# One core, clustered attention and two MLP stages: products of p and v in runs of four units instead of two

## The chip, the cores and the metric

The kernel runs on one core of one Trainium2 chip. The metric is the device time of one execution in microseconds (us). Three executions of the kernel before took 770.06, 773.00 and 773.85 us, a median of 773.0 us. The profile is of one more execution, which took 773.44 us.

## The reference

Attention over 2 batches of 8 heads, 768 queries and keys of width 64, masked by clusters; then a stage of four matrix products, then a stage of two with a leaky activation. Cut to what matters:

```python
scores = q @ k.T / 8                      # per batch and head, 768 x 768
scores = where(q_cluster == k_cluster, scores, -1e9)
p = exp(scores - max(scores))             # row by row
x = (p / sum(p)) @ v                      # 768 x 64 per head
x = x, heads side by side                 # 1536 x 512
h = ((x @ w1) * (x @ w2)) @ w3 @ w_out
g = h @ w_in;  g = max(g, 0) + alpha * min(g, 0)
out = g @ w_out2
```

The inputs are fp32. Products that must keep fp32 precision are done as three fp32r products of high and low halves (`mm3`), or as fp32 matmuls.

## The kernel before, in words

Attention is cut into 96 **units** (`NU`): unit i is 128 queries of one head against all 768 keys, six units to a head, so two heads' outputs share one tile of x. Two units with the same head in sequence make a **pair** g = i // 2. One loop (L762) over i from 0 to 103 writes the order of work of all engines by hand, as a software pipeline. Each engine runs its own instructions in the order in which the loop emits them. In iteration i:

- TensorE: `emit_T(i-4)`, six 128x128 transposes of p through PSUM tiles `t` (two tiles of three transposes, L551); `emit_S(i+1)`, four matmuls of the scores (L511, L512) into one of two `s` tiles; in some iterations a step of filling work (below); and at the end of each even iteration from 6 on `emit_PV(g)` with g = (i-6)/2: 12 products, 24 matmul instructions in the trace (L568). These have 64-column weights, and the two units of the pair sit in the two column halves of the array (`tile_position`). They accumulate in the one tile `o`, which has a PSUM bank of its own.
- ScalarE (ACT): in odd iterations from 7 on first `emit_x((i-7)//2)`, a copy of the pair's first 64 partitions of `o` into x (L580); then `emit_evac(i-4)`, the copy of the first `t` tile (L558); then `emit_exp(i)`, exp with its row sums (L526).
- VectorE (DVE): the other half of `emit_x` (L581), in even iterations `emit_r` (L533, L534: reciprocals of the row sums of a pair), the copy of the second `t` tile (L559), and `emit_max(i+1)` (L519).
- GpSimd (POOL): `emit_norm(i-2)` (L537), which scales p by the reciprocals; at the first unit of each head also the split of the next head's q and k (`h_split`, L470 to L475).
- SyncE (SP) issues the DMAs, in order: the pieces of `h_split` (L481 to L490), `v_load` (L456) behind the last pair of every second head, the weights (L142, L153), and the raw data of the mask jobs (`j_load`, L314).

A **step of filling work** is one step of `fill_steps` (L699). Up to iteration 55 these steps are the cluster mask jobs (`job`, L316): squares on ACT (L327), products (L337, L346), a sqrt (L374), transposes (L365, L381, L406), a maximum and compares on DVE (L390, L396). They come in every iteration up to 23, in odd ones up to 39, in every one from 41 to 55. From iteration 57 on, in odd iterations, they are steps of the first product with w1 and w2 for the first batch (`l1`): twelve matmuls, with a copy on ACT (L627) behind steps of w1 and a product on DVE (L631) behind steps of w2. In even iterations `w_goal` may add one step of the conversion of a weight: ACT (L185, L196, L280), DVE (L198), POOL (L281).

What limits the run-ahead: `t` has two tiles and both are used in each iteration, so `emit_T(i-3)` needs the copies of `emit_evac(i-4)`; `s` has two tiles, so `emit_S(i+2)` needs `emit_exp(i)`. The transposed p (`pth`) has three buffers of a pair each. `v` has two.

After the loop come the rest of the first product for the first batch, that of the second batch, and the later stages, which the change does not touch.

Of the kernel before, what the change touches and what calls it, by code (L numbers as in the profile page):

```python
# [8 lines left out]
F32 = mybir.dt.float32  # L9
# [7 lines left out]
B, H, S, D, NCL = 2, 8, 768, 64, 16  # L17
P = 128
# [10 lines left out]
def kernel(  # L29
# [14 lines left out]
    nc = tc.nc  # L44

    cp = ctx.enter_context(tc.tile_pool(name="cp", bufs=1))
# [258 lines left out]
    def pst(tag, shape, name, bufs=1):  # L305
        return ps.tile(shape, F32, tag=tag, name=name, bufs=bufs)
# [146 lines left out]
    def v_load(p):  # L453
        if p < B * 4:
            VS[p] = ap.tile([P, 2, NT, D], F32, tag="vs", bufs=2, name=f"vs{p}")
            nc.sync.dma_start(out=VS[p], in_=vv[p // 4, p % 4])  # L456
# [39 lines left out]
    NU = B * H * NT  # L496
    scp, pt, sums, pth, ob, XR = {}, {}, {}, {}, {}, {}

    def unit(i):
        return i // NT, i % NT  # L500
# [21 lines left out]
    def emit_exp(i):  # L522
        if i % 2 == 0:
            sums[i // 2] = ap.tile([P, 2], F32, tag="sums", bufs=3, name=f"su{i}")
        p = ap.tile([P, S], F32, tag="p", bufs=6, name=f"p{i}")
        nc.scalar.activation(  # L526
            out=p.rearrange("p (a k) -> p a k", a=2), in_=scp.pop(i)[:, :, 0:HS], func=AF.Exp,
            bias=nmax.pop(i), scale=1.0, accum_out=sums[i // 2][:, i % 2 : i % 2 + 1],
        )
        pt[i] = p  # L530
# [30 lines left out]
    def emit_PV(g):  # L561

        u, qt = unit(2 * g)
        ob[g] = pst("o", [P, P], f"o{g}")
        v = VS[u // 2]
        for kt in range(NT):
            for j in range(2):
                nc.tensor.matmul(  # L568
                    ob[g][64 * j : 64 * j + 64], lhsT=v[:, u % 2, kt], rhs=pth[g][:, kt, j * P : j * P + P],
                    start=(kt == 0), stop=(kt == NT - 1), tile_position=(0, 64 * j),  # L570
                )

    def emit_x(g):
        u, qt = unit(2 * g)
        o = ob.pop(g)
        p = u // 2
        if u % 2 == 0 and qt == 0:
            XR[p] = cp.tile([P, S], F32, tag=f"xr{p % 4}", name=f"xr{p}")
        mine = slice(0, 64) if u % 2 == 0 else slice(64, 128)
        nc.scalar.copy(out=XR[p][mine, qt * P : qt * P + P], in_=o[0:64])  # L580
        nc.vector.tensor_copy(XR[p][mine, qt * P + P : qt * P + 256], o[64:128])  # L581
        pth.pop(g)


    def lc(f, alloc, between):
# [49 lines left out]
    with tc.manual_schedule():  # L635
# [22 lines left out]
        for j in range(2):  # L658
            nc.vector.tensor_scalar(
                out=cpd[:, j], in0=ct, scalar1=cn2, scalar2=evod[:, j : j + 1], op0=ALU.mult, op1=ALU.mult  # L660
            )
        t = pst("s", [P, 2, 512], "cnt", bufs=2)[:, 0]
# [99 lines left out]
        for i in range(NU + 8):  # L762
            if 0 <= i - LT < NU:
                emit_T(i - LT)
            if i + 1 < NU:
                emit_S(i + 1)

            if i >= 7 and i % 2 == 1 and (i - 7) // 2 < NU // 2:
                emit_x((i - 7) // 2)
            if i >= 2 and i % 2 == 0 and i // 2 - 1 < NU // 2:  # L770
                emit_r(i // 2 - 1)
            if 0 <= i - 2 < NU:
                emit_norm(i - 2)
            if 0 <= i - LT < NU:
                emit_evac(i - LT)
            if i + 1 < NU:
                emit_max(i + 1)
            if i < NU:
                emit_exp(i)
                u, j = unit(i)  # L780
                for k in ((0,), (1, 2), (3, 4), (), (5,), ())[j]:
                    h_split(u + 1, k)
            if i >= NU or i % 2 == 1 or i < 24 or 40 < i < 56:
                if fill_at[0] < (L1_B if i < NU else L1_D):
                    if next(fill) is not None:
                        fill_at[0] += 1
            fine[0] = i < NU - 1
            if 10 <= i < 54 and i % 2 == 0:
                w_goal(at["l1", 0, 2, 0])
            if NUH + 8 <= i < NU - 1 and i % 2 == 0:  # L790
                w_goal(at["l1", 0, fill_at[0] // 4, 0] + 3)
            if NUH + 4 <= i < NUH + 8:
                x_split(0, i - NUH - 4, 0)
                x_split(0, i - NUH - 4, 1)
                xdone.append(i)
            if i == NU - 1:
                late.append(i)
                for k in range(2):
                    w = st_tile(f"wo{k}").rearrange("p a n -> p (a n)").rearrange("p (g t n) -> p g t n", g=3, t=2)
                    for g in range(3):  # L800
                        WO[3 * k + g] = w[:, g, 0], w[:, g, 1]
            if i >= NU - 1:
                w_goal(at["wo", 0, 3, 0])

            k = i - 6
            if k >= 0 and k % 2 == 0 and k // 2 < NU // 2:
                emit_PV(k // 2)
                if k % 12 == 10:
                    v_load(k // 12 + 2)
        pscope.close()  # L810


# [59 lines left out]
        for b, a in ((0, 0), (0, 1), (1, 0), (1, 1)):  # L872
            s = slice(a * HS, a * HS + HS)
            for e in range(4):
                t = alloc_c(f"l2_{b}{e}{a}")
# [323 lines left out]
```

## Time and profile before

| | |
|---|---|
| median of three executions | 773.0 us (770.06 to 773.85) |
| the profiled execution | 773.44 us |
| its span, first to last instruction | 771.6 us |
| TensorE (PE) busy | 746.4 us, 97% |
| its weight loads (PEld) busy | 675.7 us, 88% |
| VectorE busy | 464.6 us, 60% |
| ScalarE busy | 458.0 us, 59% |
| GpSimd busy | 270.1 us, 35% |
| share of the chain that ended last on PE | 86% |
| granted TensorE clock, mean | 0.99 |

The profiled execution is 0.44 us over the median. Between its span and its time lie 1.8 us. A row of the timeline gives the start in us from the first instruction, the length in us, engine, line, operation, output and inputs, shapes and how many instructions were merged; in brackets stands how long the engine was idle before it, and what ended that. Matmuls overlap: the distance from one start to the next is what one costs, not its length.

### The profile page before, as it was taken

How to read it: one execution, taken by the hardware profiler on the slowest of the kernel's cores; microseconds unless marked ns; L12 is line 12 of the kernel's file. 1: busy time of each engine (PE TensorE's matmuls, PEld its weight loads, DVE VectorE, ACT ScalarE, POOL GpSimd, SP SyncE). 2: the span in 40 equal slices, each digit the busy share in tenths (PEclk: the TensorE clock that was granted, in tenths of full speed). 3: DMA queues.
4: the chain of work that ended last, by engine and by line, in shares of the span. 5: the costliest groups of instructions: out<-in, count | busy, mean ns of one | idle time of the engine just before them, and what ended most of it. 6: DMA issues, size and time to landing. Idle time of an engine off the chain costs nothing.

```text
span 771.6 us, 13292 instructions
## 1 busy us (share of the span) xinstructions
PE 746.4 (97%) x5025; PEld 675.7 (88%) x5025; DVE 464.6 (60%) x807; ACT 458.0 (59%) x946; POOL 270.1 (35%) x244
## 2 busy tenths in 40 slices
PE   5899999989999999999999999999999999999998
PEld 2787788879999989999999999999989998989886
DVE  3776798995666674357233446525645547776764
ACT  5687887675556675467344657647565544555443
POOL 0366576684555643243222432312211111221110
PEclk9799999999999999999999999999999999999999
DMA  7657466253534635756444497756655226433402
GB/s 251 193 177 224 108 173 166 67 123 79 150 110 135 186 119 168 236 217 223 160 164 164 161 316 251 282 181 231 206 201 164 110 110 232 177 114 135 163 0 82
DMA packets 39440, 129.41 MB, mean 168 GB/s; under 512 B 5232, under 2 KB 5360, under 8 KB 39376
## 3 DMA queue, kind: packets, MB, share of 16 engines
q1 hardware_dynamic: 39376, 128.56, 51.5%
q8 instruction: 40, 0.66, 0.3%
q14 instruction: 24, 0.20, 0.1%
HBM read 86.17 MB, written 28.31 MB: 148 GB/s over the span
## 4 chain that ended last, share of the span: by engine, by line
PE 86%; DMA 5%; DVE 3%; POOL 2%; ACT 2%; issue 1%; SPq 1%; POOLq 0%; ACTq 0%; DVEq 0%
PE o L568 6%; PE t L551 6%; PE l L298 6%; PE l L299 6%; PE acc L300 6%; PE acc L299 6%; PE l L300 6%; PE acc L298 6%; PE s L511 3%; PE s L512 3%; PE l1a L299 3%; PE l1b L298 3%; PE l1a L298 3%; PE l1a L300 3%; PE l1b L300 3%; PE l1b L299 3%
## 5 line engine op out<-in xcount | busy, mean ns | idle before, releaser
L281 POOL TENSOR_TENSOR wh<-wt,wh 128x512 fp32r<-128x512 f32 x57 | 74.2, 1301 | 169.7 <-ACT wh L280 165.0
L537 POOL TENSOR_SCALAR p<-p,su 128x768 f32<-128x768 f32 x96 | 88.4, 929 | 91.8 <-DVE su L534 42.4
L198 DVE SCALAR_TENSOR_TENSOR wt<-wu,wt 128x512 uint32<-128x512 uint32 x72 | 72.9, 1013 | 40.9 <-ACT wt L196 40.7
L519 DVE TENSOR_REDUCE nm<-s 128x1 f32<-128x768 f32 x96 | 91.5, 953 | 8.6 <-PE s L512 3.1
L526 ACT ACTIVATE p<-s,nm 128x768 f32<-128x768 f32 x96 | 87.1, 907 | 6.8 <-DVE nm L519 5.4
L551 PE MATMUL t<-cst,p 128*128 128x128 f32 x576 | 84.1, 281 | 3.6 <-DVE pt L559 1.6
L551 PEld LDWEIGHTS t<-cst,p 128*128 128x128 f32 x576 | 65.9, 143 | 15.8 <-issue 7.9
L511 PE MATMUL s<-st 128*128 128x384 f32 x192 | 74.9, 390 | 2.0 <-ACT p L526 1.5
L568 PE MATMUL o<-pt,vs 128*64 128x128 f32 x1152 | 73.5, 277 | 0.0
L568 PEld LDWEIGHTS o<-pt,vs 128*64 128x64 f32 x1152 | 61.9, 137 | 12.3 <-issue 12.1
L512 PE MATMUL s<-st 80*128 80x384 f32 x192 | 66.7, 347 | 0.2 <-DMA st<-mk 0.2
L558 ACT COPY pt<-t 128x384 f32<-128x384 f32 x96 | 45.9, 478 | 30.4 <-PE t L551 29.4
L559 DVE COPY pt<-t 128x384 f32<-128x384 f32 x96 | 52.8, 550 | 16.1 <-PE t L551 15.1
L244 POOL TENSOR_TENSOR sp<-sx,sp 128x512 fp32r<-128x512 f32 x16 | 22.4, 1420 | 107.9 <-ACT sp L241 107.5
L968 DVE SCALAR_TENSOR_TENSOR gr<-gr,alp 128x384 f32<-128x384 f32 x32 | 20.9, 652 | 49.1 <-ACT gr L967 49.1
L196 ACT ACTIVATE wt<-wr 128x512 uint32<-128x512 uint32 x72 | 48.3, 671 | 0.0
L185 ACT ACTIVATE wu<-wr 128x512 f32<-128x512 f32 x72 | 47.9, 666 | 0.0
L298 PE MATMUL l1a<-xs,wh 128*128 128x384 f32 x128 | 43.3, 338 | 1.3 <-DVE pr L631 0.7
L280 ACT CAST wh<-wt 128x512 fp32r<-128x512 f32 x57 | 35.4, 621 | 13.1 <-DVE wt L198 7.1
L298 PE MATMUL l1b<-xs,wh 128*128 128x384 f32 x128 | 43.1, 337 | 0.0
L299 PE MATMUL l1a<-xs,wh 128*128 128x384 f32 x128 | 43.0, 336 | 0.1
L631 DVE TENSOR_TENSOR pr<-l1b,asb 128x384 f32<-128x384 f32 x32 | 17.8, 555 | 42.1 <-PE l1b L300 24.3
(244 smaller groups left out, 1984.9 us busy)
## 6 DMA issues: line engine op xcount, KB each, us to landing
wr<-in_w_dram SPq DMA_DIRECT2D x48, 512.0 KB, 5.3
kept<-wh SPq DMA_DIRECT2D x41, 512.0 KB, 5.8
wh<-kept SPq DMA_DIRECT2D x39, 512.0 KB, 4.0
wr<-in_w3t_dram SPq DMA_DIRECT2D x16, 512.0 KB, 4.1
ywc<-kept SPq DMA_DIRECT2D x15, 512.0 KB, 3.5
jm<-in_qka_dram SPq DMA_DIRECT2D x12, 512.0 KB, 5.6
hr<-in_qkh_dram SPq DMA_DIRECT2D x16, 384.0 KB, 3.6
st<-st SPq DMA_DIRECT2D x16, 384.0 KB, 3.7
```

Of the source, the lines that this page charges most:

```text
L198: nc.vector.scalar_tensor_tensor(out=t, in0=u, scalar=3, in1=t, op0=ALU.logical_shift_left, op1=ALU.bitwise_or)
L281: nc.gpsimd.tensor_tensor(out=lo, in0=tts.pop(n), in1=f32(hi), op=ALU.subtract)
L298: nc.tensor.matmul(o, lhsT=whi, rhs=xhi, start=first, stop=False)
L299: nc.tensor.matmul(o, lhsT=whi, rhs=xlo, start=False, stop=False)
L300: nc.tensor.matmul(o, lhsT=wlo, rhs=xhi, start=False, stop=last)
L511: nc.tensor.matmul(t[:, a, 0:HS], lhsT=s[:, 0, q], rhs=s[:, 1, ks], start=True, stop=False)
L512: nc.tensor.matmul(t[:, a, 0:HS], lhsT=s[0:80, 2, q], rhs=s[0:80, 3, ks], start=False, stop=True)
L519: nc.vector.tensor_reduce(out=m, in_=scp[i][:, :, 0:HS], op=ALU.max, axis=AX.XY, negate=True)
L526: nc.scalar.activation(out=p.rearrange("p (a k) -> p a k", a=2), in_=scp.pop(i)[:, :, 0:HS], func=AF.Exp, bias=nmax.pop(i), scale=1.0, acc ...
L537: nc.gpsimd.tensor_scalar(out=pt[i], in0=pt[i], scalar1=sums[i // 2][:, i % 2 : i % 2 + 1], scalar2=1.0, op0=ALU.mult, op1=ALU.mult)
L551: nc.tensor.transpose(t[:, k], pt[i][:, kt * P : kt * P + P], ident)
L568: nc.tensor.matmul(ob[g][64 * j : 64 * j + 64], lhsT=v[:, u % 2, kt], rhs=pth[g][:, kt, j * P : j * P + P], start=(kt == 0), stop=(kt == N ...
```

## The change

`emit_PV` of two pairs, that is of four units, comes at the end of every fourth iteration (8, 12, ... 100) in place of one pair at the end of every second. Both pairs write halves of one `o` tile. `emit_x` is called once per run, in the iteration after it, and copies both pairs with one instruction per engine where they are of one head (16 of the 24 runs) and with two where they are of two (8 runs). In that iteration `emit_exp(i)` is emitted ahead of `emit_x` and `emit_evac`. `v_load` stays in the same iterations.

```diff
     def emit_PV(g):
 
         u, qt = unit(2 * g)
-        ob[g] = pst("o", [P, P], f"o{g}")
+        if g % 2 == 0:
+            ob[g // 2] = pst("o", [P, 2, P], f"o{g}")
         v = VS[u // 2]
         for kt in range(NT):
             for j in range(2):
                 nc.tensor.matmul(
-                    ob[g][64 * j : 64 * j + 64], lhsT=v[:, u % 2, kt], rhs=pth[g][:, kt, j * P : j * P + P],
+                    ob[g // 2][64 * j : 64 * j + 64, g % 2], lhsT=v[:, u % 2, kt], rhs=pth[g][:, kt, j * P : j * P + P],
                     start=(kt == 0), stop=(kt == NT - 1), tile_position=(0, 64 * j),
                 )
 
-    def emit_x(g):
-        u, qt = unit(2 * g)
-        o = ob.pop(g)
-        p = u // 2
-        if u % 2 == 0 and qt == 0:
-            XR[p] = cp.tile([P, S], F32, tag=f"xr{p % 4}", name=f"xr{p}")
-        mine = slice(0, 64) if u % 2 == 0 else slice(64, 128)
-        nc.scalar.copy(out=XR[p][mine, qt * P : qt * P + P], in_=o[0:64])
-        nc.vector.tensor_copy(XR[p][mine, qt * P + P : qt * P + 256], o[64:128])
-        pth.pop(g)
+    def emit_x(n):
+        o = ob.pop(n)
+        parts = []
+        for k in range(2):
+            u, qt = unit(4 * n + 2 * k)
+            p = u // 2
+            if u % 2 == 0 and qt == 0:
+                XR[p] = cp.tile([P, S], F32, tag=f"xr{p % 4}", name=f"xr{p}")
+            x = XR[p][0:64] if u % 2 == 0 else XR[p][64:128]
+            parts.append((u, x.rearrange("p (t q) -> p t q", q=P), qt, k))
+            pth.pop(2 * n + k)
+        if parts[0][0] == parts[1][0]:
+            (_, x, qt, _) = parts[0]
+            parts = [(x[:, qt : qt + 4].rearrange("p (k j) q -> p k j q", j=2), slice(0, 2))]
+        else:
+            parts = [(x[:, qt : qt + 2].rearrange("p (k j) q -> p k j q", j=2), slice(k, k + 1)) for _, x, qt, k in parts]
+        for x, k in parts:
+            nc.scalar.copy(out=x[:, :, 0], in_=o[0:64, k])
+        for x, k in parts:
+            nc.vector.tensor_copy(x[:, :, 1], o[64:128, k])
...
-            if i >= 7 and i % 2 == 1 and (i - 7) // 2 < NU // 2:
-                emit_x((i - 7) // 2)
+            if i % 4 == 1:
+                if i < NU:
+                    emit_exp(i)
+                if i >= 9:
+                    emit_x((i - 9) // 4)
...
             if i < NU:
-                emit_exp(i)
+                if i % 4 != 1:
+                    emit_exp(i)
...
-            k = i - 6
-            if k >= 0 and k % 2 == 0 and k // 2 < NU // 2:
-                emit_PV(k // 2)
-                if k % 12 == 10:
-                    v_load(k // 12 + 2)
+            if i % 4 == 0 and 8 <= i < NU + 8:
+                for g in (i // 2 - 4, i // 2 - 3):
+                    emit_PV(g)
+                    if g % 6 == 5:
+                        v_load(g // 6 + 2)
```

## Rows read from the trace of the kernel before

**Rows 1.** Windows of the attention loop: us, busy us (instructions) by engine, clock, DMA

```profile
39.00:172.00 133.00, 124.98 (x1268) 106.44 (x1267) 110.14 (x208) 103.77 (x227) 89.10 (x86) 1.00 0.55 150
172.00:275.00 103.00, 103.00 (x898) 95.68 (x897) 66.05 (x126) 60.00 (x136) 55.79 (x55) 1.00 0.50 135
```

**Rows 2.** Timeline of PE, 273.7 to 280 us, iterations 89 to 91

```profile
273.75 0.93 PE L568 MATMUL o<-pt,vs 128*64 128x128 f32 x14
...
275.86 0.34 PE L512 MATMUL s<-st 80*128 80x384 f32 x1
276.05 0.82 PE L551 MATMUL t<-cst,p 128*128 128x128 f32 x6
276.63 0.44 PE L511 MATMUL s<-st 128*128 128x384 f32 x1
...
277.26 0.34 PE L512 MATMUL s<-st 80*128 80x384 f32 x1
277.52 1.53 PE L568 MATMUL o<-pt,vs 128*64 128x128 f32 x24
278.99 0.88 PE L551 MATMUL t<-cst,p 128*128 128x128 f32 x6
279.62 0.42 PE L511 MATMUL s<-st 128*128 128x384 f32 x1
```

**Rows 3.** Line 568, then line 551's first idle entry: durations, idle us and times

```profile
L568 PE MATMUL o<-pt,vs x1152: 272/273/324, 39.4 to 306.9; 128*64 128x128 f32 x192
...
  issue: 12.1, 47
...
  issue: 7.9, 40
```

**Rows 4.** Lines 580 and 581, the copies of x: min/median/max ns

```profile
L580 ACT COPY xr<-o x48: 238/258/261, 41.0 to 307.4; 64x128 f32<-64x128 f32 x48
...
L581 DVE COPY xr<-o x48: 292/294/296, 41.3 to 307.7; 64x128 f32<-64x128 f32 x48
```

**Rows 5.** Timeline of PE: five waits, in iterations 12, 19, 24, 32 and 44

```profile
53.28 0.64 PE L337 MATMUL ja<-jm,cst 128*32 128x256 f32 x8 [0.46 <-ACT jm L327]
...
75.68 0.64 PE L337 MATMUL ja<-jm,cst 128*32 128x256 f32 x8 [1.46 <-ACT pr L352]
...
90.27 0.44 PE L511 MATMUL s<-st 128*128 128x384 f32 x1 [0.90 <-ACT p L526]
...
109.00 0.55 PE L551 MATMUL t<-cst,p 128*128 128x128 f32 x3 [0.70 <-DVE pt L559]
...
139.73 0.55 PE L406 MATMUL jd<-cst,pr 128*128 128x128 f32 x3 [0.87 <-DVE pr L396]
```

**Rows 6.** Timelines of ACT, SP and DVE: what stands behind these waits

```profile
52.17 1.06 ACT L327 ACTIVATE jm<-jm 128x1024 f32<-128x1024 f32 x1 [0.37 <-DMA jm<-in_qka_dram]
...
67.33 0.33 SPq L456 DMA_DIRECT2D vs<-in_vv_dram  x1
...
74.09 1.06 ACT L327 ACTIVATE jm<-jm 128x1024 f32<-128x1024 f32 x1 [2.71 <-DMA jm<-in_qka_dram]
...
87.93 1.28 ACT L526 ACT_TABLE_LOAD   x1
...
106.74 1.29 DVE L198 SCALAR_TENSOR_TENSOR wt<-wu,wt 128x512 uint32<-128x512 uint32 x1
...
138.32 1.82 DVE L396 TENSOR_TENSOR pr<-pr,mx 128x384 f32<-128x384 f32 x2
```

**Rows 7.** Timelines of PE and ACT, iteration 66, behind a step of w1

```profile
200.87 0.82 PE L551 MATMUL t<-cst,p 128*128 128x128 f32 x6
...
202.02 0.47 ACT L558 COPY pt<-t 128x384 f32<-128x384 f32 x1
202.38 0.91 ACT L526 ACTIVATE p<-s,nm 128x768 f32<-128x768 f32 x1
```

**Rows 8.** Timeline of DVE, iteration 90: the copy of the second `t` tile

```profile
277.40 0.54 DVE L559 COPY pt<-t 128x384 f32<-128x384 f32 x1
```

## The prediction

> **What bounds the kernel now.** I read the windows first, to see how much room each stage has, then the timeline of TensorE, then what ended its waits.
>
> In the loop's first part (39 to 172 us, iterations 6 to 56) TensorE is busy 124.98 of 133 us, with VectorE at 110.14 and ScalarE at 103.77: three engines close together, and 8.0 us in which TensorE waits. In the second part (172 to 275 us, filled up with steps of w1 and w2) it is busy all 103.00 us, and VectorE only 66.05 [rows 1]. TensorE sets the pace; in the first part its partners are just behind. The granted clock is 1.00 in both, its upper level.
>
> The timeline shows what one run of PV costs. S ahead of T starts its last matmul 0.19 us before T (275.86 to 276.05); ahead of PV it is 0.26 (277.26 to 277.52). PV to the next T is 1.47 (277.52 to 278.99). T to S is 0.63 behind PV and 0.58 elsewhere [rows 2]. Inside a run, 14 instructions last 0.93 us and one lasts 0.273, so seven pairs have six distances of 0.11 us, and twelve pairs stream in 1.31 us [rows 2, 3]. A run that stands alone therefore takes 0.07 + 1.47 + 0.05 = 1.59 us for 1.31 us of streaming. The other **0.28 us** is getting into the 64-column arrangement and out again.
>
> The Trainium skill, "TensorEngine Tiling (Array Packing)", section "Key Properties", says that changing the tiling mode (not just the tile) drains the engine. If each change let one matmul run out, that would be 2 x (0.273 - 0.11) = 0.33 us, an estimate by that page's rule, and 24 such changes would be worth 7.9 us. The trace agrees in kind, and gives the smaller number.
>
> **The change part by part.** The profiled execution is the basis, 773.44 us, 0.44 above the median.
>
> *Fewer runs.* 48 runs become 24. 24 x 0.28 = **-6.7 us**, if TensorE is never kept waiting longer. Bounds: nothing, if the pause belongs to the start of each pair's accumulation rather than to the switch (no row shows two pairs in sequence); and 24 x (12.1/47 + 7.9/40) = 24 x 0.455 = -10.9 us, if all of the weight loader's idle time around runs went [rows 3]. I take the first, since it is the distance between starts on the pacing engine.
>
> *The copies of x.* ACT's 48 copies of 0.258 us become 32, DVE's 48 of 0.294 likewise [rows 4]. A copy twice as wide lies between one and two of these. Both engines gain something between 0 and 4.7 us (16 x 0.294) over the loop, off the path except where named below. In the split runs two copies follow each other, which puts the copy of `t` back by under 0.1 us. Taken as nothing.
>
> *exp ahead of x.* In iterations 1, 5, 9, ... exp(i) no longer stands behind the wait for PV and for T; its maximum was emitted an iteration before, so it runs under the double run, which lasts 2.8 us. Without this move x would hold exp up by the second half of the run. On the path I count nothing: what TensorE asks of ACT next is the copy of `t`, which stands behind x as before.
>
> *One bank, buffers, queues.* The next run writes `o` four iterations after x has read it. pth has three buffers; a run frees two, and the next is written two iterations on. Both hidden. v_load follows the same pair as before. What is queued behind it on SP still waits for the end of that run; POOL keeps its order. The last run is in iteration 100 as before, and TensorE has filling work there, so what the loop gains or loses is the kernel's.
>
> *The cover that moves.* This is the price. The loop had T S T S PV; now it has T S T S T S T S and PV twice. Of four iterations, call them A, A+1, A+2, A+3 (A the one after a run), the PV that stood at the end of A+1 is now at the end of A+3. It covered 1.6 us in which ACT and DVE did A+1's work before TensorE asked for it in A+2 and A+3. Wherever TensorE waits in A+2 or A+3 for something on a clock of its own, it now arrives 1.59 us earlier, waits that much longer, and does the PV afterwards.
>
> - *Five such waits stand in the trace*, all in A+2 or A+3, 0.46 to 1.46 us each [rows 5]. The square at 52.17 waits for a DMA. The one at 74.09 waits 2.71 us for a DMA that was queued on SP behind v_load, and v_load, at 67.33, for the end of a run. exp(23) stands behind a table load at 87.93. The copy of `t` that T waits for at 109.00 stands behind a weight conversion of 1.29 us, and L406 behind two compares that took 1.82 [rows 6]. If all wait the full 1.59 longer: +8.0. In the last four a copy of x (0.26 or 0.29) leaves the delaying engine's queue: -1.1. **+6.9 us.** Lower bound nothing, if the delayed work moves ahead with TensorE.
> - *The second part.* Eight groups have a step of w1 in A. In A+1 ACT then first does that step's copy, and in five of the eight a weight conversion, so that the copy of `t` starts 1.15 us after T (200.87 to 202.02) and ends at 202.49; exp ends at 203.29 [rows 7]. With no PV there, the next T would start at 200.87 + 0.58 for T + 0.82 for S (276.63 to 277.26 and 0.19) = 202.27 [rows 2]. It waits to some 202.5, and the S behind it, due at 203.1, to some 203.4 for exp. That is +0.6 in each of the five, and I take 0.1 in the other three: **+3.3 us**. Bounds: 0, and 8 x 0.6 = 4.8.
> - *The other eleven groups.* Iteration 90 is the pattern. The reciprocals delay the copy of `t` to 277.40, and it ends at 277.94 [rows 8]. With no PV, T would start at 277.26 + 0.19 = 277.45 and its second half 0.29 later, so it waits 0.2. I add as much for the exponential behind it. Against this, DVE and ACT have 1.3 us more to catch up under the double run, and of the present short waits some go. I take 0.25 per group, **+2.8 us**; bounds 0 and 0.4.
>
> Sum: -6.7 + 6.9 + 3.3 + 2.8 = +6.3; 773.44 + 6.3 = 779.7, against the median 773.0 + 6.3 = 779.3. I say **779.0 us**.
>
> The conversion and the compares on DVE that stand behind two of the waits took 1.29 and 1.82 us [rows 6]; each has two SBUF inputs. The Trainium skill, "GPSIMD Engine Reference", section "1. Specifications", says that GpSimd shares its SBUF interfaces with VectorE and that they contend where a VectorE instruction has two SBUF inputs. By it these stretches hang on what POOL does at the time and would not shrink when TensorE comes sooner; the rows quoted show their lengths, not POOL's part in them.
>
> **The rivals.** What a measurement of this kernel can tell from no change is about 0.5%, 3.9 us.
>
> - *The cover was not needed.* DVE and ACT catch up under the double run, the five waits follow TensorE, and the slack in A+2 and A+3 is over 1.6 us. Then only the first term is left: 773.0 - 6.7 = 766.3 us. For it: in the second part VectorE is busy 64% of the time [rows 1]. Against it: the waits that are there [rows 5] and ACT's lateness behind a step of w1 [rows 7]. It decides the sign from the point where extra waits stay under 6.7 us in all, 0.28 per group. Chance 0.14.
> - *The five waits do not grow*, because what TensorE waits for is itself released by TensorE's earlier instructions, but the other two prices are right: -6.7 + 3.3 + 2.8 = -0.6, 772.4 us. Or they grow by half: 775.8. For it: L396 and the compares depend on transposes of an iteration before. Against it: a DMA, a table load and a conversion do not. Chance 0.30.
> - *The run has no gain to give.* The pause comes with each pair's new accumulation, so a double run costs 3.2 us in place of 2.9. Then the waits alone are left: 773.0 + 13.0 = 786 us. Against it: T starts a new tile after three transposes without a pause in its 0.58 us [rows 2]. Chance 0.04.
>
> **How the numbers follow.** My forecast has 0.52, by itself 776 to 784. Faster by over 0.5% is the first rival, 0.14; within 0.5% the second, 0.30; slower the forecast and the third, 0.56. The range goes from 769.5, which leaves out most of the first rival, to 784.5, which leaves out the third and the upper tail of the forecast.
>
> **What would show it.** Right: runs of 48 matmuls with one pair distance of 0.11 between the two pairs; S to PV still 0.26, PV to T twice 1.31 plus 0.16; L568's idle on issue 23 times, some 6 us; TensorE's waits at L337, L406 and at the T and S of A+2 and A+3 grown by 1 us and more; S of A+2 waiting for exp in five groups of the second part; DVE's wait for ACT's copy of x fewer. Wrong: the second part shorter than before by 2 us or more, or the five waits no longer than they were, or a pause in the middle of a run.

## The result: 1.2% slower, and the profile after

| | before | after |
|---|---|---|
| median | 772.48 us (4 runs) | **781.66 us** (4 runs) |
| lowest, highest | 770.06, 773.85 | 780.62, 782.83 |
| ratio, 95% interval | | **1.0123** [1.0092, 1.0154] |
| span of the profiled execution | 771.6 | 779.3 |
| TensorE busy in it | 746.4 of 771.6 | 744.8 of 779.3 |

The changed kernel is slower by 9.2 us. TensorE's busy time hardly moved, and the span grew: most of the loss is waiting.

The windows of the changed kernel (window, length, then busy time of PE, PEld, DVE, ACT, POOL, granted clock, DMA share, GB/s), beside [rows 1]:

```profile
0.00:39.00 39.00, 25.65 (x197) 16.21 (x197) 22.04 (x48) 25.71 (x49) 11.10 (x17) 1.00 0.71 220
39.00:172.00 133.00, 120.50 (x1196) 102.86 (x1196) 99.96 (x189) 97.56 (x207) 81.49 (x80) 0.99 0.53 145
172.00:275.00 103.00, 101.16 (x882) 94.25 (x883) 66.42 (x122) 59.71 (x133) 58.06 (x57) 1.00 0.49 130
```

In the loop's first part TensorE waits 133.00 - 120.50 = 12.5 us where it waited 8.0. In the second part, where it had waited for nothing, it now waits 1.84 us.

A better ruler than windows is the distance between first transposes (T) of a group, iterations A to A+3, because it doesn't slide when the loop is late. Worked out from the starts of the T rows of both traces, in us:

| groups of iterations | before | after | difference |
|---|---|---|---|
| the five with a wait priced in the prediction: 9-12 | 10.35 | 11.45 | +1.10 |
| 17-20 | 14.34 | 14.73 | +0.40 |
| 21-24 | 11.07 | 13.81 | +2.73 |
| 29-32 | 9.99 | 10.81 | +0.82 |
| 41-44 | 10.53 | 11.85 | +1.31 |
| second part with a step of w1, five of eight (65-68, 73-76, 77-80, 81-84, 85-88) | 12.88 each | 13.17 to 13.28 | +0.29 to +0.40 each |
| the other three (57-60, 61-64, 69-72) | 12.88 each | 12.69 to 12.70 | -0.18 to -0.19 each |
| ten others: 5-8, 13-16, 25-28, 33-36, 37-40, 45-48, 49-52, 53-56, 89-92, 93-96 | | | +0.60, +0.12, +0.53, -0.11, +0.45, +0.10, +0.68, -0.89, +0.87, +0.45 |

From the first T of iteration 9 to that of iteration 97 the loop grew by 9.7 us. The two profiled spans differ by only 7.7, because the changed kernel's loop starts 2.4 us earlier (T of iteration 5 at 33.02, before at 35.46): in the profiled execution of before, TensorE ran part of the first 39 us at a lower clock, 0.82 on average against the 1.00 above:

```profile
0.00:39.00 39.00, 27.35 (x185) 19.37 (x186) 20.39 (x45) 24.11 (x45) 8.72 (x14) 0.82 0.70 220
```

**What the change was made of did happen.** TensorE's timeline in iteration 68 of the changed kernel (start, duration, engine, line, operation, tiles, shape, count):

```profile
212.54 0.34 PE L512 MATMUL s<-st 80*128 80x384 f32 x1
212.80 2.84 PE L569 MATMUL o<-pt,vs 128*64 128x128 f32 x48
215.57 0.88 PE L551 MATMUL t<-cst,p 128*128 128x128 f32 x6
...
  issue: 6.4, 24
```

The last line is from the view of what the weight loader waited for at L569. A run of 48 lasts 2.84 us, against 1.53 for one of 24: the second pair adds 1.31, exactly its streaming time, so there is no pause in the middle. S to the run is 0.26 as before. The weight loader idles 24 times, 6.4 us in all, where it idled 47 times and 12.1 us [rows 3]. So the switches that were to go are gone.

**Where the time went.** TensorE's waits of the changed kernel at the five places of [rows 5], with those just beside them and the run behind one of them (in brackets: us waited, what ended it):

```profile
51.22 0.64 PE L337 MATMUL ja<-jm,cst 128*32 128x256 f32 x8 [0.62 <-ACT jm L327]
74.28 0.64 PE L337 MATMUL ja<-jm,cst 128*32 128x256 f32 x8 [2.23 <-ACT pr L352]
87.65 0.98 PE L551 MATMUL t<-cst,p 128*128 128x128 f32 x6 [1.01 <-ACT pt L558]
89.86 0.44 PE L511 MATMUL s<-st 128*128 128x384 f32 x1 [1.23 <-ACT p L526]
91.04 4.16 PE L569 MATMUL o<-pt,vs 128*64 128x128 f32 x48
108.99 0.55 PE L551 MATMUL t<-cst,p 128*128 128x128 f32 x3 [1.02 <-DVE pt L559]
111.54 0.55 PE L551 MATMUL t<-cst,p 128*128 128x128 f32 x3 [0.62 <-DVE pt L559]
141.40 0.55 PE L551 MATMUL t<-cst,p 128*128 128x128 f32 x3 [0.66 <-ACT pt L558]
143.91 0.55 PE L406 MATMUL jd<-cst,pr 128*128 128x128 f32 x3 [1.26 <-DVE pr L396]
```

L337 waits 0.62 (before 0.46) and 2.23 (1.46), S of iteration 24 waits 1.23 (0.90) with a new wait of 1.01 just ahead of it, T of iteration 32 (at 111.54) waits 0.62, a little less than before (0.70), with a new 1.02 in T of iteration 31 ahead of it (at 108.99), and L406 waits 1.26 (0.87) with a new 0.66 ahead of it. What held them up (ACT, then DVE):

```profile
72.70 1.06 ACT L327 ACTIVATE jm<-jm 128x1024 f32<-128x1024 f32 x1 [2.44 <-DMA jm<-in_qka_dram]
...
87.52 1.28 ACT L526 ACT_TABLE_LOAD   x1
88.82 0.90 ACT L526 ACTIVATE p<-s,nm 128x768 f32<-128x768 f32 x1
...
105.28 0.43 DVE L593 COPY xr<-o 64x256 f32<-64x256 f32 x1 [1.45 <-ACT xr L591]
...
107.19 1.02 DVE L396 TENSOR_TENSOR jm<-jm,mx 128x384 f32<-128x384 f32 x2
...
108.40 0.54 DVE L559 COPY pt<-t 128x384 f32<-128x384 f32 x1
```

Iteration 24 shows the mechanism best. The changed kernel comes to the transposes of L381 at 86.15, where before was there at 87.98, since the run that before had at 85.1 to 86.6 is missing: 1.8 us sooner. The exponential behind its table load starts at 88.82 and lets S go at 89.86, where before's S started at 90.27 [rows 5]: 0.4 us sooner. The other 1.4 us have gone into the waits of 1.01 and 1.23, and the run is still to be done. At 108.99 it is a copy of `t` again, but one an iteration earlier. It stands behind two compares (107.19), which before ran at 104.21, mostly under the run of iteration 30 that is now missing, and these behind a copy of x that waited 1.45 us for ACT's. And in the group 9-12 only 0.16 us are at L337; another 0.54 is a wait of S for the transfer of a mask, which before doesn't have.

In the second part, iteration 66 is the pattern that the prediction drew from [rows 7]. TensorE, then ACT:

```profile
205.88 0.82 PE L551 MATMUL t<-cst,p 128*128 128x128 f32 x6
207.44 0.84 PE L551 MATMUL t<-cst,p 128*128 128x128 f32 x6
208.45 0.44 PE L511 MATMUL s<-st 128*128 128x384 f32 x1 [0.16 <-ACT p L526]
...
206.08 0.48 ACT L638 COPY asb<-l1a 128x384 f32<-128x384 f32 x1 [2.67 <-PE l1a L300]
206.46 0.68 ACT L185 ACTIVATE wu<-wr 128x512 f32<-128x512 f32 x1
207.04 0.47 ACT L558 COPY pt<-t 128x384 f32<-128x384 f32 x1
207.40 0.91 ACT L526 ACTIVATE p<-s,nm 128x768 f32<-128x768 f32 x1
```

The copy of `t` stands behind w1's copy and a conversion and starts 207.04 - 205.88 = 1.16 us after T, as before (1.15). T to the next T is 1.56 here, against 1.40 (0.58 for T and 0.82 for S) where nothing is late, and S waits 0.16 for the exponential.

The other way round it shows at T of iteration 57, which stands behind a run and waits for POOL's normalization (before, then the changed kernel):

```profile
171.58 0.88 PE L551 MATMUL t<-cst,p 128*128 128x128 f32 x6 [1.13 <-POOL p L537]
...
176.97 0.88 PE L551 MATMUL t<-cst,p 128*128 128x128 f32 x6 [0.26 <-POOL p L537]
```

With a second pair in the run ahead of it the wait is 0.87 us shorter; the group 53-56, which ends with it, is the one that got 0.89 shorter.

### The profile page after: what moved, and what is told of

It is laid out like the page before. It is cut to its first block, busy times and chain, and to the rows that moved or that the text cites. A ratio compares the mean times of both kernels' runs of the same rounds, so it can differ in the third digit from the quotient of the medians.

```text
span 779.3 us, 13249 instructions
## 1 busy us (share of the span) xinstructions
PE 744.8 (96%) x5025; PEld 673.9 (86%) x5025; DVE 459.2 (59%) x791; ACT 455.0 (58%) x930; POOL 269.8 (35%) x244
## 4 chain that ended last, share of the span: by engine, by line
PE 83%; DVE 7%; ACT 4%; DMA 3%; issue 1%; POOL 1%; SPq 1%; ACTq 0%; DVEq 0%
PE o L569 7%; PE l L298 6%; PE l L299 6%; PE acc L300 6%; PE acc L299 6%; PE l L300 6%; PE acc L298 6%; PE t L551 5%; PE l1a L299 3%; PE l1b L298 3%; PE l1a L298 3%; PE l1a L300 3%; DVE nm L519 3%; PE l1b L300 3%; PE l1b L299 3%; PE s L511 3%
## 5 line engine op out<-in xcount | busy, mean ns | idle before, releaser
L569 PE MATMUL o<-pt,vs 128*64 128x128 f32 x1152 | 69.5, 278 | 0.0
L569 PEld LDWEIGHTS o<-pt,vs 128*64 128x64 f32 x1152 | 63.7, 139 | 6.4 <-issue 6.4
L559 DVE COPY pt<-t 128x384 f32<-128x384 f32 x96 | 52.6, 548 | 11.1 <-PE t L551 10.1
L638 ACT COPY asb<-l1a 128x384 f32<-128x384 f32 x32 | 15.3, 479 | 51.1 <-PE l1a L300 51.1
```

The lines of the kernel that those rows point to most:

```text
L569: nc.tensor.matmul(ob[g // 2][64 * j : 64 * j + 64, g % 2], lhsT=v[:, u % 2, kt], rhs=pth[g][:, kt, j * P : j * P + P], start=(kt == 0), s ...
```

## The experiments

Theory: the switches are worth some 0.28 us each; the PV of A+1, moved to the end of A+3, was cover for late partners of TensorE, and the waits that it uncovers cost more than the switches give. Rivals: the price lies in the copies of x or in the exponential put ahead of them; or in the five waits alone.

### Two iterations later

```diff
-            pth[g] = ap.tile([P, NT, 256], F32, tag="pth", bufs=3, name=f"pt{g}")
+            pth[g] = ap.tile([P, NT, 256], F32, tag="pth", bufs=4, name=f"pt{g}")
...
-            if i % 4 == 0 and 8 <= i < NU + 8:
-                for g in (i // 2 - 4, i // 2 - 3):
+            if i % 4 == 2 and 10 <= i < NU + 8:
+                for g in (i // 2 - 5, i // 2 - 4):
```

Against the changed kernel; the exponential and the copies of x that went first in 4n+1 go first in 4n+3.

> The changed kernel with its double runs two iterations later: pairs 2n and 2n+1 at the end of iteration 4n+10 in place of 4n+8, x and the early exp in the iteration after; pth gets a fourth buffer, since a pair now stays two iterations longer. Theory (cover): the five fixed waits of iterations 12, 19, 24, 32 and 44 then stand in the first or second iteration behind a double run, which is done ahead of them, so they do not grow; the steps of w1 in iterations 57, 61, ... come two iterations behind a run and their late copy of t is covered by the next one. The 6.7 us of fewer switches stay, less some 2 us of other short waits: 767 to 771 us, second part 2 us shorter than before, no stretch at the half clock. Rival (any double run starves TensorE, since T S four times over is faster than ACT and DVE can follow, wherever it is put): 779 to 783 us, as the changed kernel. Rival (the switch costs nothing on the path): 773 us.

Measured: 778.21 us, 1.006 [1.004, 1.0079] of before. The five groups with the priced waits came to -0.9 us together against before (in the changed kernel +6.4), and seven groups of the second part took 12.65, 0.23 less than before. So far the theory. But the time missed, since other groups of the first part got longer: 25-28 by 1.9, 37-40 by 1.4, 53-56 by 0.9. TensorE's timeline, and the window behind it:

```profile
174.31 0.87 PE L551 MATMUL t<-cst,p 128*128 128x128 f32 x6 [2.08 <-POOL p L537]
...
175.60:179.00 3.40, 3.40 (x12) 3.40 (x11) 1.38 (x4) 0.67 (x2) 2.91 (x4) 0.50 0.62 118
```

T of iteration 57 waits 2.08 us for POOL's normalization: with no run ahead of it the wait that was 1.13 and 0.26 lies bare. The granted clock is then 0.50 for 3.4 us, and the group that starts there is 1.3 longer than before. Moving the runs moves the cover, and what it leaves bare depends on the place: the first part has such steps at both places tried.

### The filling shifted by one

```diff
-            if i >= NU or i % 2 == 1 or i < 24 or 40 < i < 56:
+            if i != 57 and (i >= NU or i % 2 == 1 or i < 24 or 40 < i < 56):
```

Against the changed kernel: the steps of w1 come two iterations later in their groups, with the run's cover behind them.

> The changed kernel with one edit: the step of filling work of iteration 57 is left out there, so every step of w1 and w2 moves two iterations back, and steps of w1 with their copy on ACT fall in iterations 59, 63, ... (third of a group, covered by the double run of the fourth). Theory: the five groups of the second part that became 0.34 us longer become 0.19 shorter like the other three: 5 x 0.53 = 2.7 us less than the changed kernel, about 779 us; iteration 66's copy of t starts 0.6 us behind T. Rival (these groups are longer for DVE's sake, or for three steps without PV as such): as the changed kernel, 781.7.

Measured: 779.93 us, 1.0088 [1.0068, 1.0108]. All seven groups from 61 to 88 take 12.69, where the changed kernel has 13.17 to 13.28 in five of them. The timeline of TensorE and ACT in iteration 70:

```profile
220.27 0.82 PE L551 MATMUL t<-cst,p 128*128 128x128 f32 x6
...
220.85 0.48 ACT L558 COPY pt<-t 128x384 f32<-128x384 f32 x1 [3.05 <-PE t L551]
```

The copy of `t` now starts 0.58 us after T, in place of 1.16. So the excess of the five groups goes with that delay. The conversions move with the steps of w1, so which of the two delays the copy more isn't told apart. The other 0.19 per group below before is what fewer switches give here. Some of the gain is lost again behind it: the group 89-92 is 1.2 us longer than in the changed kernel.

### The exponential back behind the copies of x

```diff
             if i % 4 == 1:
-                if i < NU:
-                    emit_exp(i)
                 if i >= 9:
                     emit_x((i - 9) // 4)
...
             if i < NU:
-                if i % 4 != 1:
-                    emit_exp(i)
+                emit_exp(i)
```

> The changed kernel with exp(i) of iterations 1, 5, 9, ... back behind x and the copy of t, as it was before. Theory: exp would then start about 1.0 us behind T in place of under the double run, its s tile comes free at 1.9 us, and S of the next iteration, due at 2.0 us, waits by 0 to 0.2 us: 0 to +4 us on the changed kernel, 782 to 786 us. Rival (the move itself is what costs, since x and the copy of t wait behind exp): 2 us or more faster than the changed kernel, under 780.

Measured: 781.95 us, 1.0121 [1.0098, 1.0145]: the changed kernel again. With double runs the order of exp and x is worth nothing that can be told, either way.

### The copies and the exponential without the double runs

```diff
-            if i % 4 == 0 and 8 <= i < NU + 8:
-                for g in (i // 2 - 4, i // 2 - 3):
-                    emit_PV(g)
-                    if g % 6 == 5:
-                        v_load(g // 6 + 2)
+            if i % 2 == 0 and 6 <= i < NU + 6:
+                g = i // 2 - 3
+                emit_PV(g)
+                if g % 6 == 5:
+                    v_load(g // 6 + 2)
```

Against the changed kernel: single runs where before had them, shared tile of `o`, x copied every fourth iteration, early exponential.

> The change without its merged runs: one pair per run at the end of every second iteration as before, but both pairs in one o tile, x copied once per two runs and exp(i) ahead of it in every fourth iteration. Theory (the run's place is all): as before, 770 to 774 us, faster by at most 1 us for 16 copies less on each engine; the five waits as long as before. Rival (the wide copy, the shared tile or the early exp costs): 775 us or more.

Measured: 780.25 us, 1.0094 [1.0076, 1.0113], a miss of 6 us. The timeline of ACT, DVE and TensorE in iteration 9:

```profile
44.81 0.90 ACT L526 ACTIVATE p<-s,nm 128x768 f32<-128x768 f32 x1 [1.39 <-DVE nm L519]
45.70 0.35 ACT L591 COPY xr<-o 64x256 f32<-64x256 f32 x1
45.95 0.47 ACT L558 COPY pt<-t 128x384 f32<-128x384 f32 x1
...
46.08 0.43 DVE L593 COPY xr<-o 64x256 f32<-64x256 f32 x1 [1.31 <-ACT xr L591]
...
44.27 0.87 PE L551 MATMUL t<-cst,p 128*128 128x128 f32 x6
46.57 1.13 PE L551 MATMUL t<-cst,p 128*128 128x128 f32 x6 [0.72 <-ACT pt L558]
```

The exponential at the head of ACT's queue waits 1.39 us for its maximum, and everything behind it waits with it: x, DVE's x behind ACT's, and the copy of `t` that TensorE wants next (1.68 us after T, where it can be 0.58). This suggested that the early exponential was the price, which the next kernel tries.

### The same with the exponential in its old place

```diff
             if i % 4 == 1:
-                if i < NU:
-                    emit_exp(i)
                 if i >= 9:
                     emit_x((i - 9) // 4)
```

Against the kernel above; its other half, the condition behind which the remaining exponentials stood, goes too, so that all are where before has them.

> As e4_x_alone (single runs, one o tile per two runs, x copied once per two runs), but exp(i) back behind x and the copy of t. What e4_x_alone showed and my theory did not say: behind a single run of 1.5 us exp is not ready, ACT's x stands behind it, and DVE's x, copy and maximum stand behind ACT's x. Theory: without the early exp this is gone, 771 to 774 us, as before. Rival (the wide copy or the shared tile is what cost e4_x_alone its 7 us): 778 us or more.

Measured: 772.16 us, 0.9987 [0.9973, 1.0002]. The shared tile and the wider copies of x cost nothing. The early exponential costs 780.25 - 772.16 = 8.1 us with single runs; with double ones it costs nothing, as the third experiment shows. The run that gives it its cover is also what makes the waits.

### The double run cut in two

```diff
                 emit_T(i - LT)
+            if i % 4 == 0 and 8 <= i < NU + 8:
+                emit_PV(i // 2 - 4)
             if i + 1 < NU:
                 emit_S(i + 1)
...
-                for g in (i // 2 - 4, i // 2 - 3):
-                    emit_PV(g)
+                g = i // 2 - 3
+                emit_PV(g)
...
```

Against the changed kernel: in the same iteration, one pair ahead of S and one behind it. It adds one pair of switches per group and puts the first pair ahead of one S.

> The changed kernel with its double run cut in two in the same iteration: the first pair ahead of the scores of i+1, the second behind them, so that 48 runs and their changes of arrangement are back and nothing else moves far. Theory: 24 x 0.28 = 6.7 us on top of the changed kernel, about 788 us; in the second part the groups that took 12.70 take 12.98 (+0.28). Rival (a run's edges cost nothing where others are late): as the changed kernel in the first part and 2 us more in the second, 784 us. Rival (no price at the edges at all): 781.7 us.

Measured: 786.46 us, 1.0183 [1.0154, 1.0212], 4.8 us more than the changed kernel. The two traces differ by 2.8 between the first T of iteration 9 and that of 97, and by 2.1 ahead of it, where only one cut lies. TensorE's timeline in iteration 64, and at L406 in iteration 44:

```profile
199.45 0.82 PE L551 MATMUL t<-cst,p 128*128 128x128 f32 x6
200.19 1.53 PE L569 MATMUL o<-pt,vs 128*64 128x128 f32 x24
201.66 0.44 PE L511 MATMUL s<-st 128*128 128x384 f32 x1
...
202.56 1.53 PE L569 MATMUL o<-pt,vs 128*64 128x128 f32 x24
...
144.68 0.49 PE L406 MATMUL jd<-cst,pr 128*128 128x128 f32 x3
```

In the second part each cut costs (93.80 - 91.52) / 7 = 0.33 us per group (first T of iteration 61 to that of 89). That is the price of a switch there and back, and it bears the prediction's 0.28 out. In the first part the cut kernel is no longer than the changed one (132.33 against 133.42 from iteration 9 to 57), but that doesn't make the switch free there. The changed kernel's trace holds a stretch at half clock worth 1.3 us (last section), the cut one's none. And the first pair, now ahead of S, is cover again: L406 (144.68) and S of iteration 24 don't wait any more, and the five groups with priced waits are 2.1 us longer than before in place of 6.4. The seven other groups between iterations 9 and 57 take 3.1 us more than in the changed kernel, 0.45 each. So there the cut costs something too; what the switch costs and what the moved pair covers can't be told apart.

### Double runs in the second part alone

Before's code up to iteration 56; from there the runs of the first experiment:

```diff
-            k = i - 6
-            if k >= 0 and k % 2 == 0 and k // 2 < NU // 2:
-                emit_PV(k // 2)
-                if k % 12 == 10:
-                    v_load(k // 12 + 2)
+            if i % 2 == 0 and 6 <= i < 58:
+                gs = (i // 2 - 3,)
+            elif i % 4 == 2 and 62 <= i < NU + 8:
+                gs = (i // 2 - 5, i // 2 - 4)
+            else:
+                gs = ()
+            for g in gs:
+                emit_PV(g)
...
```

Against before; four buffers of pth, x copied per run, exponentials in their old place.

> The kernel before up to iteration 57; from there double runs as in e1_two_later (pairs 2n and 2n+1 at the end of iteration 4n+10, four pth buffers, x once per run in the iteration after), exp in its old place. Theory: where TensorE alone sets the pace the merged run is worth its 0.23 us per group: the first part as before, seven to eight groups of the second part 12.65 in place of 12.88, the end as before: 1 to 2 us less than before, 771 to 772 us. Rival (what the runs give is lost again at the part's edges): 773 us or more.

Measured: 772.27 us, 0.999 [0.9978, 1.0002]. Seven groups take 12.65, 0.23 less each: 1.6 us. The group of iterations 93 to 96 takes 0.5 more. What is left, 0.7 us in the medians, is at the edge of what 12 runs resolve.

### Weight conversions taken out of the first part

Two kernels, before and the changed one, each without the goal that spreads conversions of w1 over iterations 10 to 53:

```diff
-            if 10 <= i < 54 and i % 2 == 0:
-                w_goal(at["l1", 0, 2, 0])
```

If the waits of the first part are these conversions, the pair stand closer together than the kernels do with them.

> The kernel before without the weight conversions of iterations 10 to 53 (they are done when the first product needs them, from iteration 57 on, so a wait appears there). To be read against e9_after_late_w, by the first part alone (iterations 9 to 57): with the conversions it takes 126.2 us before and 133.4 changed, a price of 7.2. Theory: here some us less than 126.2.

> The changed kernel without the weight conversions of iterations 10 to 53, against e8_before_late_w. Theory (the partners' work that lost its cover is the price): the conversions of iterations 10, 18, 22, 26, 30 and 34 are gone, so the first part (iterations 9 to 57) is only some 3 to 4 us longer than in e8_before_late_w in place of 7.2. Rival (mask jobs and the chain of maximum, exp and copies alone make the price): still 6 us or more longer.

Measured: before without them 775.81 us, 1.0038 [1.0021, 1.0055]; the changed kernel without them 787.37, 1.0168 [1.0138, 1.0199]. From iteration 9 to 57 the first takes 123.35 us and the second 130.89, 7.5 more; with the conversions it is 126.19 and 133.42, 7.2 more. The theory put to the pair falls: the first part's price doesn't hang on conversions in DVE's and ACT's queues. Each of the two differences holds one stretch at half clock: some 1.3 us in the changed kernel's group 21-24, and some 1.6 without the conversions in the group 41-44 (+2.96 in place of +1.31). Without them both are near 5.9.

### Five runs put back

```diff
+            alone = (12, 20, 24, 32, 44)
+            gs = ()
             if i % 4 == 0 and 8 <= i < NU + 8:
-                for g in (i // 2 - 4, i // 2 - 3):
-                    emit_PV(g)
+                gs = (i // 2 - 3,) if i in alone else (i // 2 - 4, i // 2 - 3)
+            elif i + 2 in alone:
+                gs = (i // 2 - 3,)
+            for g in gs:
+                emit_PV(g)
...
```

Against the kernel of the third experiment: in the five groups of the priced waits alone, the runs stand single and where before had them. The other 19 stay double.

> The changed kernel with exp(i) in its old place (worth nothing there, e3_exp_old) and with the runs of iterations 12, 20, 24, 32 and 44 taken apart again: there, and only there, the first pair's products stand at the end of iteration 10, 18, 22, 30 and 42, as before. Theory (cover, at the five places of the prediction): these five groups are as long as before within 0.2 us each, 6.4 us less than in the changed kernel, the others as in the changed kernel: 775 to 776 us, no half clock around 90 us. Rival (e1_two_later's lesson: the late work only moves on): the groups behind them get longer, and the whole stays over 778 us.

Measured: **776.53 us**, 1.0065 [1.0047, 1.0084], 5.1 less than the changed kernel. The five groups are +0.22, -0.06, -0.15, -0.13 and 0.00 us against before. TensorE's timeline at iterations 22 to 24, where the changed kernel has its waits of 1.01 and 1.23:

```profile
84.16 1.53 PE L569 MATMUL o<-pt,vs 128*64 128x128 f32 x24
89.16 0.44 PE L511 MATMUL s<-st 128*128 128x384 f32 x1 [0.98 <-ACT p L526]
```

The run at 84.16 is back, the wait for the exponential is 0.98 as before (0.90), and the price of these five is gone. Some of it came back next door: 25-28 is 0.76 longer than before and 33-36 0.86 (in the changed kernel 0.53 and -0.11). The second part, whose code is the changed kernel's, is within 0.1 us of it.

### What works, together

The copies of x of the fifth experiment in the first part, and the double runs of the second part; against the kernel of the fifth experiment, which also gets the runs and the four buffers of the kernel with double runs in the second part alone:

```diff
-            if i % 4 == 1:
-                if i >= 9:
-                    emit_x((i - 9) // 4)
+            if i % 4 == 1 and 9 <= i < 61:
+                emit_x((i - 9) // 4)
+            if i % 4 == 3 and i >= 63:
+                emit_x((i - 11) // 4)
...
```

> What held up, together: x copied once per two single runs up to iteration 57 (e5_x_exp_old), double runs from there two iterations later (e7_second_part), exp in its old place. Theory: the two gains add, 0.8 and 0.7 us: 771 to 772 us against 773.0; second part 12.65 per group, first part within 0.5 us of e5_x_exp_old. Rival: either gain was noise, 773 us.

Measured: **771.61 us**, 0.9986 [0.9976, 0.9997], the lowest median of all, 1.1 us below before's of the same round. It is below the 0.5% that the prediction set as what can be told, though its interval just excludes 1. Its windows, beside [rows 1] and those of the changed kernel:

```profile
39.00:172.00 133.00, 125.16 (x1265) 106.73 (x1262) 108.94 (x200) 102.41 (x218) 89.03 (x86) 1.00 0.56 150
172.00:275.00 103.00, 102.97 (x908) 98.13 (x906) 68.15 (x126) 60.73 (x136) 56.30 (x56) 1.00 0.54 145
```

TensorE is busy throughout the second part again, and does 908 matmuls in the 103 us where the changed kernel did 882 and before 898. From iteration 9 to 57 the trace takes 126.20 us, as before's 126.19: the gain that the trace shows is that of the double runs, and of the copies of x it shows none.

## Why the prediction was right, and what it mis-sized

**The sign and its mechanism were right.** The kernel is slower because a run of PV was also cover. 779.0 was said, 6.0 over before, and 781.66 measured, 9.2 over. Term by term:

- *Fewer runs, -6.7 said.* The size, 0.28 us per switch there and back, is borne out where TensorE alone sets the pace: 0.33 for each one added (the cut run), 0.19 to 0.23 net for each one taken out (the shifted filling, the runs two later). No pause came in the middle of a run. What it is worth in the first part no run shows by itself. The Trainium skill, "TensorEngine Tiling (Array Packing)", section "Key Properties", speaks of a drain at a change of tiling mode. The prediction's estimate by that rule, 0.33, has the size that the cut run shows in the second part; the runs show the price there, not what makes it.
- *Five waits, +6.9 said.* Net of five switches the prediction had +5.5, and the five groups grew by 6.4. Putting the five runs back took the five groups to before's lengths and 5.1 us out of the median: **shown**. The parts were less even than said. The group 21-24 has 2.73, of which some 1.3 is a stretch at half clock (last section), which the prediction did not have; and half of what 9-12 grew is a wait that it did not name. That the sum comes so close is in part luck. The group 17-20 has only 0.40: the prediction blamed a transfer queued behind v_load. Groups 17-20 and 21-24 vary: in the trace of the shifted filling, whose first part is the same program, they are -0.96 and +1.13, and the five together 5.5, a stretch at half clock in 41-44 included.
- *Second part, +3.3 said.* Right in place and size. The prediction's net is 0.6 - 0.28 = +0.32 in five groups and 0.1 - 0.28 = -0.18 in three, together +1.1; measured are +0.29 to +0.40 in five and -0.18 to -0.19 in three, together +1.2. The shifted filling took the five away: **shown**.
- *The other eleven groups, 0.25 each.* **This is the term that was mis-sized.** Net of the switch they should have been -0.03 each; ten of them measure +2.8 together, 0.28 each, so with a switch at 0.28 the price was 0.56. The eleventh, the end from iteration 97 on, is 0.2 us shorter than before. The prediction took iteration 90 for the pattern, in which reciprocals delay one copy [rows 8]. But that iteration's own group, 89-92, grew by 0.87, and 93-96 by 0.45: nearly half of the +2.8. (The kernels with the exponential back and with the five runs put back have +0.86 and +0.43 there.) What it left out stands one iteration on (VectorE before, then TensorE, VectorE and TensorE in the changed kernel):

```profile
278.72 1.28 DVE L198 SCALAR_TENSOR_TENSOR wt<-wu,wt 128x512 uint32<-128x512 uint32 x1
...
283.97 1.11 PE L551 MATMUL t<-cst,p 128*128 128x128 f32 x6
...
285.27 1.28 DVE L198 SCALAR_TENSOR_TENSOR wt<-wu,wt 128x512 uint32<-128x512 uint32 x1
...
287.07 0.55 PE L551 MATMUL t<-cst,p 128*128 128x128 f32 x3 [0.63 <-DVE pt L559]
```

A weight conversion began 0.27 us ahead of T of iteration 91, under the run (T at 278.99 [rows 2]). Now it begins 1.30 behind that T, and T of iteration 92 waits 0.63 for the copy of `t` behind it. Of the rest, 0.60 are in the group 5-8, which varies (0.61 with the filling shifted, -0.16 and +0.05 in the two kernels just named), and 0.87 in seven groups of the first part: -0.89 in 53-56, where the second pair covers a wait, and +1.76 in the other six. What stands behind these six was not taken apart.
- *Copies of x, one bank, wider copies: nothing.* Right; with single runs they give 0.13%, within the measurement.
- *Early exponential: nothing on the path.* Right in this kernel, and only there. One half of the reason was wrong: the maximum is not ready, neither with single runs nor here (about half of the 28 waits in the first of the lines below are of such exponentials). The other half carries it: the run of 2.8 us hides that wait.

The sum of what the group lengths say is 6.36 + 1.17 + 2.80 - 0.19 = +10.1 us; less the 2.4 by which the profiled execution of before came to its loop later, it is 7.7, the difference of the spans. The medians give 9.2.

**The rivals.** *The cover was not needed* falls for the first part and holds for the groups 61 to 88 once the filling is shifted. *The five waits do not grow* falls by the five runs put back. *The run has no gain* falls by the 2.84 us run and the cut. By its parts the prediction said also that VectorE would wait for ScalarE's copy of x less often. It does, 24 times in place of 29, and longer: the same view of waits of the changed kernel (engine, tile and line, what ended it: us, count, longest):

```profile
ACT p L526 <- DVE nm L519: 20.0, 28, 3.0
...
DVE xr L593 <- ACT xr L591: 42.9, 24, 3.7
```

The first of these lines had 2.8 us in 7 waits in the same view of before, and the second 27.0. An early exponential does wait at the head of its queue. What these two waits of ACT and DVE cost TensorE the view does not say; the exponential's cost nothing that the third experiment can tell.

**What stays open.** Why *this* first part leaves no place for a double run: with the runs two iterations later the five groups are no longer than before and others are. The weight conversions are excluded as the main cause there, and so are the copies of x and the exponential. How the rest divides between the jobs on the masks, the maxima and the copies of `t` was not tried.

## What to carry to other kernels

A stretch of TensorE's work that is put somewhere else is a cost saved at its edges and a cover lost at its old place; price both, group by group, before merging runs. Where TensorE alone is busy all the time the merge pays its edges (here 0.2 us per double run, for a switch of 0.3); where partners are busy 78 and 83% of the time, as in the first part here, a step that was late can cost nearly the whole run (1.3 of 1.6 us in iteration 24). A run in place of two can also cover a wait that one did not, as at T of iteration 57. An instruction put ahead in an engine's queue must find its input ready there: otherwise all behind it waits with it, as the exponential showed at 8.1 us.

## What the runs showed that was not expected

**A wait of TensorE was followed by a stretch at half clock.** In the changed kernel T waited 1.01 us and S 1.23 us between 86.6 and 89.9. Then the granted clock was 0.50, the lower of the two levels (1.2 GHz), for 3.4 us:

```profile
90.40:93.80 3.40, 3.40 (x29) 2.96 (x29) 1.99 (x3) 2.22 (x5) 3.15 (x4) 0.50 0.02 5
```

The double run that fell there took 4.16 us in place of 2.84, 1.3 us more. Before has no such stretch in this place; where it waited 0.90 for the same exponential its clock stayed 1.00:

```profile
88.00:96.00 8.00, 7.08 (x64) 5.91 (x64) 7.35 (x16) 6.71 (x13) 4.95 (x5) 1.00 0.10 22
```

Between 40 and 300 us, five of the experiments' traces show such stretches too. In the kernel with the exponential back there are two, the other from 145.0 on:

```profile
90.40:93.80 3.40, 3.40 (x22) 2.96 (x24) 2.56 (x5) 1.72 (x4) 2.67 (x4) 0.51 0.00 0
```

With the filling shifted there is one at 144.8, with the runs two later the one at 175.6 shown above, and without the conversions the changed kernel has one from 141 and a longer one from 178.8, and before one from 169.2. The changed kernel and the one with the filling shifted have the same program in the first part, and it fell in different places: so it belongs to the execution as well as to the program.

So behind a new wait of a microsecond there can come a loss as large again, in clock. It need not come: the changed kernel's waits of 2.23 at 74.28 and of 0.66 and 1.26 at 141.40 and 143.91 have no such stretch behind them, while the shifted filling's at 144.8 stands behind waits of the same 0.66 and 1.25. What decides it these runs don't show. The kernel with the five runs put back has none between 40 and 300 us. The prediction had counted waits at their own length alone.
